# Windowed attention in groups of six query blocks instead of four, with ScalarE's sums of exponentials, shared copies, loads in two parts and ranks from a table

## The chip, the core and the metric

The kernel runs on one core of a Trainium2 chip. Its engines are TensorE (PE in the profile; PEld is its weight load), VectorE (DVE), ScalarE (ACT), GpSimd (POOL) and SyncE (SP), which here only issues the DMAs. The metric is device time in microseconds of one launch: the median of three runs of the kernel before is 353.84 us (353.21 to 354.48).

## The reference

Three layers follow each other. The first is attention for 2 batches of 8 heads, 768 positions, head size 64: each position sees its neighbours closer than 16 and 24 summaries, one for each run of 32 positions (the maximum of the keys, the mean of the values).

```python
k_sum = k.reshape(B, H, nb, block, D).max(axis=3)          # block = 32, nb = 24
v_sum = v.reshape(B, H, nb, block, D).mean(axis=3)
scores_l_m = np.where(mask_l, scale * q @ k.T, -1e9)       # |i - j| < 16
scores_s = scale * einsum('bhsd,bhnd->bhsn', q, k_sum) + np.log(block)
a = softmax(concatenate([scores_l_m, scores_s], axis=-1))
attn = a @ concatenate([v, v_sum], axis=2)
# then, on x of (2, 768, 512)
h = relu(x @ w_in); u, v = halves of h; v_n = layer norm of v
x = (u * (w_spatial @ v_n + b_spatial)) @ w_out
h = relu(x @ w_in2); x = (h * sigmoid(conv3(h))) @ w_out2
```

## The kernel before

Everything after the attention is dense products in three passes of TensorE (high x high, high x low, low x high, lines 274 to 276), 1416 matmuls in all. They are called dense here; 936 of them are 512 columns wide, 480 are 256 wide.

The attention goes by pairs of heads: n = 0 to 7, four pairs for each batch. A pair has 12 query blocks of 64 rows. Each block has 96 keys in its window and 24 summaries, so 120 columns. GB = 4 blocks make a group, NG = 3 groups make a pair; there are 24 groups. A group goes through this chain (function `group`): `qk` writes masks, logarithms and scores into one of two score tiles in PSUM (TensorE, lines 402, 406, 413); `row_max` (VectorE, 417); `exps`, one ScalarE instruction for each of four half-filled tiles of 120 columns (421); `total`, a sum over 484 columns (VectorE, 424), which also takes up a column of 1e-9; `recip` (427); `normalise` (GpSimd, 430); four transposes into the PSUM tile pt (434); a copy of pt to memory (ScalarE, 452); `pv`, the product with the values, into xp (439); the high part of the result (ScalarE, 454) and its low part (VectorE, 455). The results X are the input of the dense products `f1u` and `f1v`: `f1u(0)` needs all four pairs of batch 0.

Around the groups stand, for each pair: the load of keys and queries (`load_kq`, lines 320 and 323) and of values, already laid out in windows (`vwin`, line 330, 576 KB in one DMA); the scaled key windows (GpSimd, 339); the maxima of the keys (VectorE, 344) and their spreading (347); the means of the values. In batch 0 TensorE computes the means from vwin (line 362, 12 blocks one after another), in batch 1 VectorE adds up a second load of the values (line 369). ScalarE copies them (373), GpSimd spreads them over the blocks of each group (376). Buffers alternate between pairs: pair n + 2 is loaded into the places of pair n. Beside all this the first weight matrix `w_in` is loaded and converted in eight pieces (`convert`, lines 259 to 265, then 250 and 244).

A planner (`Plan.order`) sets the order of instructions on every engine before the program is built: each step has a list of engines with a cost, a rank, and what it reads and writes; the step that can start earliest is taken, and among those within 0.1 us the one of the lowest rank. Dense work has ranks from 1000 up, so that it fills TensorE where attention has nothing ready. The chip runs each engine's instructions in that order. The DMAs stand in one queue on SyncE, in order too; an issue waits until its buffer is free.

Of the kernel before, what the change touches and what calls it, by code (L numbers as in the profile page):

```python
# [27 lines left out]
GB = 4  # L28
NG = NB // GB
MK = 4 * NK + 2 * QB + 2 * NS  # L30
# [6 lines left out]
SLOT = 1536  # L37


class Plan:  # L40

# [8 lines left out]
    def add(self, on, rank, reads=(), writes=(), lock=False, mode=None):  # L50
# [20 lines left out]
        self.work.append((on, rank, deps - {k}, lock, mode))  # L71

    def order(self):
# [13 lines left out]
        while ready:  # L87
            best = []
            for k in ready:
                on, rank, deps, lock, mode = self.work[k]  # L90
                for e in on:
                    s = free.get(e, 0.0)
                    for j in deps:
                        t, by = end[j]
                        s = max(s, t + (self.LAND if by == "Q" else 0.0 if by == e else self.HAND))
# [73 lines left out]
def block_kernel(ctx, tc, q_in, k_in, vwin, v_in, mask, runs, w_in, w_spT, b_sp, w_outT, w_in2, conv, w_out2, out):  # L169
# [8 lines left out]
    STEP = 3.0  # L178
# [59 lines left out]
    def dma(kb, fn, rank, reads=(), writes=()):  # L238
        add({"Q": (kb / 265.0, fn)}, rank, reads, writes)
# [65 lines left out]
    def e3(j):  # L305
        return es[j].ap[:, :GB * (NK + 1)].rearrange("p (b k) -> p b k", k=NK + 1)

    def st3(j):
        return sts[j].ap[:, :3 * GB].rearrange("p (b k) -> p b k", k=GB)

# [6 lines left out]
    def load_kq(n):  # L317
        j, r = n % 2, STEP * NG * n
        b, p = divmod(n, NP)
        dma(400, lambda: SP.dma_start(kts[j].f(), k_in[b, p]), r - 12, writes=[kts[j].tok()])  # L320
        cuts = [(0, 256), (256, S)] if n == 0 else [(0, S)]
        for i, (q0, q1) in enumerate(cuts):
            dma((q1 - q0) / 2, lambda q0=q0, q1=q1: SP.dma_start(qts[j].ap[:, q0:q1], q_in[b, p][:, q0:q1]), r - 9 + 1.5 * i, writes=[qts[j].tok(q0, q1)])

    def load_values(n):
        j, r = n % 2, STEP * NG * n
        b, p = divmod(n, NP)
        if b:
            dma(384, lambda: SP.dma_start(vts[j].f(), v_in[p]), r - 7, writes=[vts[j].tok()])
        dma(576, lambda: SP.dma_start(vw3(j)[:WK], vwin[b, p]), r - 6, writes=[vws[j].tok(sub="w")])  # L330

    def keys(n):

        j, r = n % 2, STEP * NG * n
        for g in range(NG):
            def win(g=g):
                t = kts[j].ap
                src = bass.AP(tensor=t.tensor, offset=t.offset + g * GB * QB, ap=[list(t.ap[0]), [QB, GB], [1, WK]])
                POOL.tensor_scalar(out=kw3(j)[:, g * GB:(g + 1) * GB, :WK], in0=src, scalar1=SCALE, scalar2=0.0, op0=ALU.mult, op1=ALU.add)

            add({"POOL": (0.5, win)}, r - 4 + STEP * g, [kts[j].tok(g * GB * QB, (g + 1) * GB * QB + 32)], [kw_tok(j, g)], lock=True)

        def top():
            DVE.tensor_reduce(out=kss[j].ap[:, :NS], in_=kts[j].ap[:, 16:16 + S].rearrange("p (n k) -> p n k", k=32), op=ALU.max, axis=AX.X)
# [5 lines left out]
        add({"DVE": (0.94, top)}, r - 4, [kts[j].tok()], [kss[j].tok()])  # L350
        add({"POOL": (0.46, lambda: put(POOL))} if n else {"DVE": (0.33, lambda: put(DVE))}, r - 3, [kss[j].tok()], [kws[j].tok(sub="s")], lock=True)

    def means(n):
# [3 lines left out]
        if not b:  # L357
            ps, m = mms[1][:NK, :128], tok("mm1")
            for g in range(NG):
# [4 lines left out]
                add({"PE": (0.97, mm)}, r + 1, [vws[j].tok(sub="w"), runs_t.tok()], [m], mode="F")  # L364
# [16 lines left out]
    def xh(b, p, lo, hi):  # L381
        return X[b][p].tok(lo, hi)
# [418 lines left out]
```

## Time and profile before

| | |
|---|---|
| median of 3 runs | 353.84 us |
| the profiled execution: time, span | 351.99 us, 350.2 us |
| TensorE busy | 336.9 us, 96% |
| VectorE, ScalarE, GpSimd busy | 237.0, 185.1, 85.4 us |
| DMA in queue q1 | 33.49 MB, 30.1% of 16 engines' span |

The span goes from the first to the last instruction of the profiled execution. A share of busy time is an average over stages: the attention, up to about 93 us, where all engines work, and the dense rest. TensorE's matmuls overlap, so what one of them costs is read from the distance between two starts, not from its duration. Rows of the timeline begin with the start and the time from start to end; rows of the chain of waits list what released the next piece of work.

### The profile page before, as it was taken

The numbers are of one execution on the slowest core, as the hardware profiler recorded it, in microseconds if no ns is written. First come the engines' busy times: TensorE is split into PE (matmuls) and PEld (weight loads), VectorE is DVE, ScalarE is ACT, GpSimd is POOL, SyncE is SP. The second block draws the span as 40 slices with busy tenths as digits, with TensorE's granted clock in tenths as the row PEclk, the third lists the DMA queues.
The fourth block names the chain that finished last, engine by engine and source line by source line (L and its number), as shares of the span: only waits on it lengthen the run. The fifth ranks groups of instructions, "written<-read, shape, count | busy, mean of one in ns | idle before, by whom it ended". The sixth has DMA issues, their size and how long they took to land.

```text
span 350.2 us, 6496 instructions
## 1 busy us (share of the span) xinstructions
PE 336.9 (96%) x2591; PEld 282.4 (81%) x2591; DVE 237.0 (68%) x400; ACT 185.1 (53%) x374; POOL 85.4 (24%) x117
## 2 busy tenths in 40 slices
PE   7899798799999999999999999999999999999996
PEld 3867675578888888888889888888888888888886
DVE  3799888787378888899896848799885343371000
ACT  3587688687444765434331444888864434451101
POOL 3789787687224002201001020000000000000000
PEclk9999999999999999999999999999999999999999
DMA  7978976622113652032321234000000000001101
GB/s 229 319 243 281 304 216 167 188 70 62 61 61 107 220 162 86 0 104 86 112 71 52 79 102 120 0 2 0 2 1 30 32 30 30 32 1 60 60 32 60
DMA packets 11262, 33.90 MB, mean 97 GB/s; under 512 B 1504, under 2 KB 2016, under 8 KB 11232
## 3 DMA queue, kind: packets, MB, share of 16 engines
q1 hardware_dynamic: 11232, 33.49, 30.1%
q8 instruction: 20, 0.33, 0.4%
q14 instruction: 10, 0.08, 0.1%
HBM read 30.34 MB, written 3.15 MB: 96 GB/s over the span
## 4 chain that ended last, share of the span: by engine, by line
PE 84%; DMA 8%; ACT 3%; DVE 2%; POOL 1%; issue 1%; SPq 0%; ACTq 0%; DVEq 0%; POOLq 0%
PE late L275 12%; PE late L274 12%; PE late L276 12%; PE mm L274 8%; PE mm L275 8%; PE mm L276 8%; DMA a<-vwin 4%; PE xp L275 3%; PE xp L274 3%; PE xp L276 3%; PE mm L362 3%; PE pt L275 3%; PE pt L274 3%; PE pt L276 3%; PE xp L439 2%; DMA a<-w_in 2%
## 5 line engine op out<-in xcount | busy, mean ns | idle before, releaser
L615 DVE SCALAR_TENSOR_TENSOR x<-x,conv_t 128x767 f32<-128x767 f32 x32 | 32.4, 1016 | 16.8 <-ACT x L612 16.6
L421 ACT ACTIVATE a<-s,a 128x120 f32<-128x120 f32 x96 | 26.7, 370 | 7.8 <-DVE a L417 7.6
L260 ACT ACTIVATE a<-a 128x512 f32<-128x512 f32 x28 | 18.9, 676 | 16.3 <-POOL a L244 5.3
L430 POOL TENSOR_TENSOR a<-a,a 128x480 f32<-128x480 f32 x24 | 23.9, 996 | 7.9 <-ACT a L421 4.7
L263 DVE SCALAR_TENSOR_TENSOR a<-a,a 128x512 uint32<-128x512 uint32 x28 | 20.4, 729 | 5.2 <-ACT a L260 4.1
L621 DVE TENSOR_TENSOR x<-x 128x768 f32<-128x768 f32 x16 | 15.3, 957 | 9.0 <-ACT x L618 8.9
L499 POOL TENSOR_TENSOR stat<-stat,mhalf 128x1 f32<-128x1 f32 x12 | 10.5, 873 | 44.8 <-DVE stat L496 44.8
L265 DVE SCALAR_TENSOR_TENSOR a<-a,a 128x512 uint32<-128x512 uint32 x28 | 20.5, 732 | 0.7
L439 PEld LDWEIGHTS xp<-a,a 120*64 120x64 f32 x384 | 13.3, 137 | 9.3 <-POOL a L376 3.0
L439 PE MATMUL xp<-a,a 120*64 120x64 f32 x384 | 16.4, 228 | 3.5 <-POOL a L376 1.7
L618 ACT ACTIVATE x<-x 128x768 f32<-128x768 f32 x16 | 13.5, 841 | 11.7 <-DVE x L615 11.7
L376 POOL TENSOR_SCALAR a<-a 24x512 f32<-24x512 f32 x24 | 16.6, 693 | 7.7 <-ACT a L373 6.2
L417 DVE TENSOR_REDUCE a<-s 128x4 f32<-128x480 f32 x24 | 15.2, 638 | 4.5 <-PE s L413 4.5
L424 DVE TENSOR_REDUCE a<-a 128x4 f32<-128x484 f32 x24 | 15.6, 649 | 2.1 <-ACT a L421 1.6
L434 PE MATMUL pt<-ident,a 128*120 128x128 f32 x96 | 15.2, 281 | 1.6 <-POOL a L430 1.5
L244 POOL TENSOR_TENSOR w<-a,w 128x512 fp32r<-128x512 f32 x9 | 11.5, 1275 | 19.1 <-ACT w L250 19.1
L640 ACT COPY tmp<-late 128x512 f32<-128x512 f32 x7 | 4.1, 587 | 22.7 <-PE late L276 22.7
L274 PE MATMUL mm<-x,w 128*128 128x256 f32 (+1 forms) x40 | 15.6, 389 | 0.3 <-ACT v L515 0.3
L455 DVE TENSOR_TENSOR x<-xp,x 128x256 fp32r<-128x256 f32 x24 | 10.0, 418 | 8.5 <-ACT x L454 8.4
L452 ACT COPY a<-pt 120x512 f32<-120x512 f32 x24 | 14.2, 594 | 2.8 <-PE pt L434 2.6
L274 PE MATMUL mm<-w,x 128*128 128x512 f32 x40 | 15.7, 392 | 0.0
L276 PE MATMUL mm<-w,x 128*128 128x512 f32 x40 | 15.6, 389 | 0.0
(295 smaller groups left out, 1075.5 us busy)
## 6 DMA issues: line engine op xcount, KB each, us to landing
a<-w_in SPq DMA_DIRECT2D x16, 512.0 KB, 4.3
a<-vwin SPq DMA_DIRECT2D x8, 576.0 KB, 6.0
a<-w_out SPq DMA_DIRECT2D x8, 512.0 KB, 3.6
a<-k_in SPq DMA_DIRECT2D x8, 400.0 KB, 3.9
out<-tmp SPq DMA_DIRECT2D x11, 256.0 KB, 2.0
a<-q_in SPq DMA_DIRECT2D x7, 384.0 KB, 6.2
tmp<-w_spT SPq DMA_DIRECT2D x6, 384.0 KB, 3.8
a<-w_outT SPq DMA_DIRECT2D x4, 512.0 KB, 3.9
```

What stands on the lines that cost most here:

```text
L260: add({"ACT": (0.68, lambda: ACT.mul(fu.f(), half(1).bitcast(F32), 2.0 ** -112))}, rank, [raw.tok()], [fu.tok()])
L263: add({"DVE": (0.69, lambda: DVE.scalar_tensor_tensor(out=last.u(), in0=fu.u(), scalar=0x80000000, in1=last.u(), op0=ALU.bitwise_and, op1= ...
L265: add({"DVE": (0.69, lambda: DVE.scalar_tensor_tensor(out=fu.u(), in0=fu.u(), scalar=3, in1=last.u(), op0=ALU.logical_shift_left, op1=ALU. ...
L274: PE.matmul(ps, lhsT=lh, rhs=rh, start=first and i == 0, stop=False)
L275: PE.matmul(ps, lhsT=lh, rhs=rl, start=False, stop=False)
L276: PE.matmul(ps, lhsT=ll, rhs=rh, start=False, stop=last and i == n - 1)
L376: POOL.tensor_scalar(out=vw3(j)[WK:NK, g * GB:(g + 1) * GB], in0=vss[j].ap[WK:NK].unsqueeze(1).to_broadcast([NS, GB, 128]), scalar1=1.0, s ...
L421: ACT.activation(out=e[:, u, :NK], in_=sv[:, u // 2, u % 2], func=AF.Exp, bias=st[:, 0, u:u + 1])
L424: DVE.tensor_reduce(out=st[:, 1], in_=e, op=ALU.add, axis=AX.X)
L430: POOL.tensor_tensor(out=e[:, :, :NK], in0=e[:, :, :NK], in1=st[:, 2].unsqueeze(2).to_broadcast([128, GB, NK]), op=ALU.mult)
L439: PE.matmul(xp[h * D:(h + 1) * D, k * QB:(k + 1) * QB], lhsT=vw3(j)[:NK, g * GB + k, h * D:(h + 1) * D], rhs=pts[:NK, 256 * h + 128 * (k / ...
L615: DVE.scalar_tensor_tensor(out=ct.f()[:, to], in0=hh.f()[:, of], scalar=conv_t[:, 3 * f + k:3 * f + k + 1], in1=ct.f()[:, to], op0=ALU.mul ...
```

## The change

GB goes from 4 to 6: 16 groups of six blocks, two for each pair. A group has three blocks side by side in each half of the score tile (GA = 3), six exponentials, six transposes in two halves of three that use the same part of pt one after the other, each half with a copy of its own. The exponentials give their sums as accumulator outputs; VectorE's `total` then adds only the sum and the 1e-9 of each block (12 numbers). Copies of pt and the high part of the result may go to ScalarE or VectorE, the normalising to GpSimd or VectorE, key windows and spreading of means to GpSimd or ScalarE, low parts of weights to VectorE or GpSimd. TensorE computes the means of pairs 0 and 1 only; from pair 2 on VectorE adds up the second load of the values. In batch 0 keys, queries and vwin are loaded in two parts each. Two tables, SHIFT and PICK, change ranks and fix the engine of single steps of the planner.

```diff
-GB = 4
+GB = 6
+GA = GB // 2
+MEANS_PE = (0, 1)
+SHIFT = (
+    "YYHDBIKKdNCAAKKdiEMucfejQJEfadUhADmQZTDURBAAqLisGARFbFNFJgVKANHhUupWfUntjlLrPsdOKtBbbEsSewBaCCFQJsWKiFsGMEAOSVAAcCoQoJfr"
...
+PICK = (
+    "------------------------01------1--------1---0------0---0-----------------10------0------0-1-0-0----------0-------------"
...
-        self.work.append((on, rank, deps - {k}, lock, mode))
+        if k < len(PICK) and PICK[k] != "-":
+            on = dict([list(on.items())[int(PICK[k])]])
+        self.work.append((on, rank + 0.5 * (SIGNS.index(SHIFT[k]) - 24 if k < len(SHIFT) else 0), deps - {k}, lock, mode))
...
-        if b:
-            dma(384, lambda: SP.dma_start(vts[j].f(), v_in[p]), r - 7, writes=[vts[j].tok()])
-        dma(576, lambda: SP.dma_start(vw3(j)[:WK], vwin[b, p]), r - 6, writes=[vws[j].tok(sub="w")])
+        if n not in MEANS_PE:
+            dma(384, lambda: SP.dma_start(vts[j].f(), v_in[b, p]), r - 7, writes=[vts[j].tok()])
+        parts = NG if n < NP and VPART else 1
+        for i in range(parts):
+            b0, b1 = NB // parts * i, NB // parts * (i + 1)
+            dma(48 * (b1 - b0), lambda b0=b0, b1=b1: SP.dma_start(vw3(j)[:WK, b0:b1], vwin[b, p][:, b0:b1]), r - 6 + 0.5 * i,
+                writes=[vws[j].tok(b0 * 128, b1 * 128, "w")])
...
-        if not b:
+        if n in MEANS_PE:
...
-                ACT.activation(out=e[:, u, :NK], in_=sv[:, u // 2, u % 2], func=AF.Exp, bias=st[:, 0, u:u + 1])
+                ACT.activation(out=e[:, u, :NK], in_=sv[:, u // GA, u % GA], func=AF.Exp, bias=st[:, 0, u:u + 1], scale=1.0, accum_out=sm[:, u, :1])
...
-            DVE.tensor_reduce(out=st[:, 1], in_=e, op=ALU.add, axis=AX.X)
+            DVE.tensor_reduce(out=st[:, 1], in_=sm, op=ALU.add, axis=AX.X)
...
-        add({"POOL": (1.02, normalise)}, r + 3.5, [st_], [e_], lock=True)
-        add({"PE": (0.46, transposes)}, r + 4.6, [e_], [tok("pt")], mode="F")
-        add({"ACT": (0.6, lambda: ACT.copy(pts[:NK], pt[:NK]))}, r + 5.1, [tok("pt")], [pts_])
-        add({"PE": (0.6, pv)}, r + 5.8, [pts_, vw_tok(j, g, "w"), vw_tok(j, g, "m")], [tok("xp")], mode="P")
-        add({"ACT": (0.4, lambda: ACT.copy(hi, xp[:, :GB * QB]))}, r + 6.5, [tok("xp")], [xh(b, p, t0, t1)])
+        add({"POOL": (1.5, normalise), **({"DVE": (0.91, lambda: normalise(DVE))} if NORM else {})}, r + 4.5, [st_], [e_], lock=True)
+        for h in range(2):
...
+            add({"PE": (0.37, lambda h=h: transposes(h))}, r + 6 + 0.5 * h, [e_], [tok("pt")], mode="F")
+            add({"ACT": (0.52, lambda copy=copy: copy(ACT)), **({"DVE": (0.53, lambda copy=copy: copy(DVE))} if FLEX else {})}, r + 6.5 + 0.5 * h, [tok("pt")], [part.tok()])
+        add({"PE": (0.88, pv)}, r + 7.5, [pts_, vw_tok(j, g, "w"), vw_tok(j, g, "m")], [tok("xp")], mode="P")
+        add({"ACT": (0.52, lambda: ACT.copy(hi, xp[:, :GB * QB])), **({"DVE": (0.53, lambda: DVE.tensor_copy(hi, xp[:, :GB * QB]))} if FLEX else {})}, r + 8.5, [tok("xp")], [xh(b, p, t0, t1)])
```

Three places show how the order moves. The first is SyncE's queue of loads in batch 0; before, a5 holds the values of pairs 1 and 3, a11 those of pairs 0 and 2, and each pair has one vwin.

```order
L330 DMA a5_0_210<-vwin 96x1536
L320 DMA a7_0_96<-k_in 128x800
L323 DMA a6_0_128<-q_in 128x768
L259 DMA a1_0_247<-w_in 128x1024
L320 DMA a13_0_99<-k_in 128x800
L259 DMA a0_0_195<-w_in 128x1024
L323 DMA a12_0_183<-q_in 128x768
L330 DMA a11_0_134<-vwin 96x1536
```

In the changed kernel a2 holds the values of pairs 0 and 2, a3 those of pairs 1 and 3; these rows go from pair 1's values to pair 2's.

```order
L380 DMA a3_0_297<-vwin 96x768 x2
L370 DMA a7_0_219<-q_in 128x384
L376 DMA a6_0_130<-v_in 128x768
L299 DMA a1_0_352<-w_in 128x1024
L299 DMA a0_0_194<-w_in 128x1024
L370 DMA a6_0_130<-q_in 128x384
L367 DMA a8_0_95<-k_in 128x800
L370 DMA a7_0_219<-q_in 128x384
L380 DMA a3_0_297<-vwin 96x768
L380 DMA a2_0_133<-vwin 96x768 x2
```

The loads come in halves; a second load of values (v_in) for pairs 2 and 3 is new in batch 0; the first half of pair 3's vwin now stands ahead of both halves of pair 2's.

The second place is TensorE at the means of pair 2; before, twelve products with vwin as their input stand between a value product (439) and the next transposes.

```order
L413 MATMUL s_0_80<-a10_0_94,a6_0_128 64x120 x8
L439 MATMUL xp_83<-a13_0_99,a5_0_210 64x64 x8
L362 MATMUL mm_1_85<-a11_0_134,a3_0_86 120x128 x12
L434 MATMUL pt_82<-ident_65,a2_0_95 120x128 x4
```

In the changed kernel one transposition of VectorE's sums stands for them, and dense products (314 to 316) follow.

```order
L476 MATMUL s_1_81<-a5_0_98,a7_0_219 64x120 x12
L497 MATMUL pt_82<-ident_65,a8_0_95 120x128 x3
L432 MATMUL xp_83<-ident_65,a12_0_86 120x128
L314 MATMUL mm_1_85<-x01_0_101,w0_0_327 128x512
L315 MATMUL mm_1_85<-x01_0_101,w0_0_327 128x512
L316 MATMUL mm_1_85<-x01_0_101,w1_0_509 128x512
```

TensorE no longer waits for vwin there, but for the smaller load of v_in by way of VectorE.

The third place is ScalarE's start; before, the exponentials of two groups are followed by copies and conversions only.

```order
L421 ACTIVATE a2_0_95<-s_0_80,a10_0_94 128x120 x4
L421 ACTIVATE a2_0_95<-s_1_81,a4_0_98 128x120 x4
L373 ACTIVATE a7_0_96<-mm_1_85 24x128
L452 COPY a7_0_96<-pt_82 120x512
L260 ACTIVATE a1_0_247<-a0_0_195 128x512
L454 CAST x00_0_97<-xp_83 128x256
```

In the changed kernel key windows (392) and the spreading of means (438) stand there too.

```order
L484 ACTIVATE a8_0_95,a4_0_94<-s_0_80,a4_0_94 128x120 x6
L484 ACTIVATE a9_0_99,a5_0_98<-s_1_81,a5_0_98 128x120 x6
L392 ACTIVATE a5_0_98<-a9_0_99 128x6x96
L300 ACTIVATE a0_0_194<-a0_0_194 128x512
L433 ACTIVATE a11_0_100<-mm_1_85 24x128
L438 COPY a2_0_133<-a11_0_100 24x768
L392 ACTIVATE a4_0_94<-a8_0_95 128x6x96
L519 COPY a10_0_96<-pt_82 120x384
```

Six exponentials now have a second output each, and three steps of GpSimd (one spreading, two windows) have come to ScalarE ahead of its first copy of pt.

## Rows read from the trace of the kernel before

**Rows 1.** The page, its first part: busy us, share, instructions.

```profile
PE 336.9 (96%) x2591; PEld 282.4 (81%) x2591; DVE 237.0 (68%) x400; ACT 185.1 (53%) x374; POOL 85.4 (24%) x117
```

**Rows 2.** Busy time by stretches: stretch, length, engines, granted clock, DMA share, GB/s.

```profile
4.90:52.30 47.40, 41.81 (x722) 33.60 (x722) 39.33 (x76) 32.16 (x94) 36.87 (x49) 1.00 0.86 272
52.30:93.20 40.90, 37.24 (x542) 28.91 (x540) 30.07 (x61) 29.18 (x83) 29.18 (x37) 1.00 0.38 107
93.20:347.30 254.10, 254.00 (x1324) 218.50 (x1320) 166.25 (x261) 122.14 (x197) 16.88 (x17) 1.00 0.19 61
```

**Rows 3.** Chain of waits, 20 to 70 us: start, length, what.

```profile
21.87 6.40 DMA a<-vwin
...
28.31 2.88 PE mm L362 x24
...
33.03 6.48 DMA a<-vwin
...
39.55 2.88 PE mm L362 x24
...
49.37 5.70 DMA a<-k_in
...
60.23 5.95 DMA a<-w_in
```

**Rows 4.** Timeline of PE, four short stretches: start, length, instructions.

```profile
9.08 2.85 PE L362 MATMUL mm<-a,a 96*120 96x128 f32 x24 [1.33 <-DVE a L424]
11.77 0.60 PE L434 MATMUL pt<-ident,a 128*120 128x128 f32 x4
12.30 0.30 PE L402 MATMUL s<-a 64*64 64x240 bf16 x4
...
13.14 0.69 PE L439 MATMUL xp<-a,a 120*64 120x64 f32 x16
13.75 0.30 PE L402 MATMUL s<-a 64*64 64x240 bf16 x4
...
24.70 0.30 PE L402 MATMUL s<-a 64*64 64x240 bf16 x4
...
25.39 0.38 PE L274 MATMUL mm<-x,w 128*128 128x256 f32 x1
...
92.62 0.69 PE L439 MATMUL xp<-a,a 120*64 120x64 f32 x16
93.23 0.50 PE L274 MATMUL mm<-w,x 128*128 128x512 f32 x1
93.57 0.39 PE L275 MATMUL mm<-w,x 128*128 128x512 f32 x1
93.80 0.39 PE L276 MATMUL mm<-w,x 128*128 128x512 f32 x1
```

**Rows 5.** Timeline of ACT, from its first exponentials.

```profile
7.17 2.12 ACT L421 ACTIVATE a<-s,a 128x120 f32<-128x120 f32 x8 [5.18 <-DVE a L417]
...
19.51 0.27 ACT L373 ACTIVATE a<-mm 24x128 f32<-24x128 f32 x1
19.80 0.68 ACT L260 ACTIVATE a<-a 128x512 f32<-128x512 f32 x1
20.50 0.59 ACT L452 COPY a<-pt 120x512 f32<-120x512 f32 x1
21.09 1.11 ACT L421 ACTIVATE a<-s,a 128x120 f32<-128x120 f32 x4
22.08 0.39 ACT L454 CAST x<-xp 128x256 fp32r<-128x256 f32 x1
22.54 0.59 ACT L452 COPY a<-pt 120x512 f32<-120x512 f32 x1
23.02 0.68 ACT L260 ACTIVATE a<-a 128x512 f32<-128x512 f32 x1
```

**Rows 6.** Groups by line: shapes, count, busy us, mean ns, idle before.

```profile
L424 DVE TENSOR_REDUCE a<-a 128x4 f32<-128x484 f32 x24 | 15.6, 649 | 2.1 <-ACT a L421 1.6 <-POOL a L430 0.2
```

More of the change, by code (lines that the diff above doesn't have):

```diff
@@ L335, in keys, with win, top @@
         for g in range(NG):
-            def win(g=g):
+            def win(eng, g=g):
                 t = kts[j].ap
                 src = bass.AP(tensor=t.tensor, offset=t.offset + g * GB * QB, ap=[list(t.ap[0]), [QB, GB], [1, WK]])
[L339 to L344, printed above, removed]
+                dst = kw3(j)[:, g * GB:(g + 1) * GB, :WK]
+                if eng is ACT:
+                    ACT.mul(dst, src, SCALE)
+                else:
+                    eng.tensor_scalar(out=dst, in0=src, scalar1=SCALE, scalar2=0.0, op0=ALU.mult, op1=ALU.add)
+            add({"POOL": (0.8, lambda win=win: win(POOL)), "ACT": (0.7, lambda win=win: win(ACT))}, r - 4 + STEP * g,
+                [kts[j].tok(g * GB * QB, (g + 1) * GB * QB + 32)], [kw_tok(j, g)], lock=True)
+        parts = 2 if n < NP and KPART else 1
+        for i in range(parts):
+            def top(i=i, w=S // parts):
+                DVE.tensor_reduce(out=kss[j].ap[:, w // 32 * i:w // 32 * (i + 1)], in_=kts[j].ap[:, 16 + w * i:16 + w * (i + 1)].rearrange("p (n k) -> p n k", k=32), op=ALU.max, axis=AX.X)
+            w = S // parts
+            add({"DVE": (0.14 + w / 960, top)}, r - 4, [kts[j].tok(16 + w * i, 16 + w * (i + 1))], [kss[j].tok(w // 32 * i, w // 32 * (i + 1))])
         def put(eng):
@@ L398, in qk @@
             for c in range(2):
-                at = NK if c == 0 and g else 2 * NK if c == 1 and g == NG - 1 else 0 if c == 0 else NK
+                at = 0 if c == 0 and g == 0 else 2 * NK if c == 1 and g == NG - 1 else NK
                 for h in range(2):
                     rows = slice(h * D, (h + 1) * D)
-                    PE.matmul(s[c * QB:(c + 1) * QB, h, :2 * NK], lhsT=one[rows], rhs=masks[rows, at:at + 2 * NK], start=True, stop=False, skip_group_check=True)
+                    PE.matmul(s[c * QB:(c + 1) * QB, h, :GA * NK], lhsT=one[rows], rhs=masks[rows, at:at + GA * NK], start=True, stop=False, skip_group_check=True)
             for c in range(2):
@@ L407, in qk @@
                               start=False, stop=True, skip_group_check=True)
-            for a in range(2):
+            for a in range(GA):
                 for c in range(2):
@@ L763 @@
             vwin[:, :, at:at + hi - lo, b, j * D:(j + 1) * D] = vh[:, :, j, lo:hi]
[L764 to L765 removed]
+    vin = pairs_T(v)
+    mask = np.zeros((QB, 5, NK), f32)
     bf16 = mybir.dt.np(mybir.dt.bfloat16)
@@ L769 @@
             inside = 1 <= c - p <= 31
-            for m, ok in enumerate((inside and c >= 16, inside, inside, inside and c < QB + 16)):
+            for m, ok in enumerate((inside and c >= 16, inside, inside, inside, inside and c < QB + 16)):
                 mask[p, m, c] = 0.0 if ok else -1.0e9
     weight = f32(math.log(32))
-    logs, three = np.zeros((QB, 2 * NS), f32), np.zeros((QB, QB), f32)
+    logs, three = np.zeros((QB, GA * NS), f32), np.zeros((QB, QB), f32)
     for r in range(3):
@@ L781 @@
         runs[16 + j * 32:48 + j * 32, j] = 1.0 / 32.0
-    mask = np.concatenate([mask.reshape(QB, 4 * NK), np.eye(QB, dtype=f32), three, logs], axis=1)
+    mask = np.concatenate([mask.reshape(QB, 5 * NK), np.eye(QB, dtype=f32), three, logs], axis=1)
     mask = np.concatenate([mask, mask], axis=0).astype(bf16)
```

135 lines of the change are left out of this document (88 added, 47 removed).

## The prediction, on record before the changed kernel ran

> **What bounds the kernel now.** I read the page's busy shares first, then busy time by stretches, the chain of waits, and the timelines of TensorE and ScalarE. TensorE is busy 96% of the span [rows 1]. The stretches say where the other 4% lie: from 93.2 to 347.3 us it is busy 254.0 of 254.1 us; from 4.9 to 52.3 us it is idle 47.40 - 41.81 = 5.6 us, from 52.3 to 93.2 us 40.90 - 37.24 = 3.7 us [rows 2]. 52.3 is where batch 0's attention ends, 93.2 where the last value product does. [...] In the first stretch VectorE is busy 39.3 us, GpSimd 36.9, ScalarE 32.2, and the DMA engines 86% at 272 GB/s: everything is near its limit and nothing is at it. The chain of waits tells why TensorE waits there: twice a vwin takes 6.4 and 6.5 us from issue to landing, and 2.88 us of means stand behind each [rows 3]. Later a k_in (5.7 us) and a w_in (6.0 us) do the same, in the second stretch.
>
> So the time follows from P, the end of the last value product (93.2 now), and the dense work that is left then, which runs without a gap. By the order 1320 of the 1416 dense matmuls are left now and 1284 in the changed kernel. A matmul of 512 columns takes 0.23 us from start to start [rows 4], so 36 fewer shorten the rest by 8.3 us. No change of time means P = 93.2 + 8.3 = 101.5 us.
>
> **The change, part by part, on TensorE up to P.** Busy time there is 41.8 + 37.2 = 79.0 us, before it 4.9 us.
> - Means of pairs 2 and 3: two sets of twelve blocks go. A set takes 11.77 - 9.08 = 2.69 us [rows 4]: -5.4 us. Two more transpositions of sums, 0.13 us each at the rate of the four at 11.77: +0.3.
> - Transposes: 96 as before, but 32 batches of three for 24 of four. Four take 0.53 us with one change of layout [rows 4]. At a cost per transpose nothing changes; at a cost per batch it is 8 x 0.53 = +4.2. I take +1.5, nearer the first, since a matmul's price in these rows goes by its columns.
> - Scores: four blocks take 25.39 - 24.70 = 0.69 us [rows 4]. 16 groups of six at 1.04 or 24 of four at 0.69 are both 16.6 us; were the cost one per group, 5.5 us would go. I take 0, the value by columns. Value products (13.75 - 13.14 = 0.61 for four) by the same rule: 0.
> - 36 more dense matmuls ahead of P: +8.3.
> - The start: mask and first queries are larger; I take +0.3 us, a DMA of 0.1 MB at 272 GB/s.
>
> Work up to P is then 4.9 + 79.0 - 5.4 + 0.3 + 1.5 + 8.3 + 0.3 = 88.9 us, and P = 88.9 + idle. Against 101.5 the change of time is idle - 12.6 us. With today's idle of 9.3 us that is -3.3; so the question is TensorE's idle time in the new attention.
>
> **Idle in batch 0.** It ends with the eighth value product. TensorE's own work up to there: 4.9 + 41.8 - 5.4, with some 0.7 for transposes, 1.0 for one batch of scores more (66 blocks ahead for 60), 1.0 for six dense matmuls with their changes of layout: 44.0 us. ScalarE is the engine that gains work. From its first exponentials at 7.2 us to the last copy of the eighth group its order holds 54 exponentials (nine groups), 4 scalings and 3 casts of weights, 4 copies of means, 12 copies of 384 columns, 3 key windows and 4 spreadings. Four exponentials take 22.08 - 21.09 = 0.99 us, a scaling 0.70, a copy of means 0.29, a copy of 512 columns 0.48 (22.54 to 23.02), so one of 384 about 0.40 [rows 5]; a cast is priced as a scaling; the windows (576 columns) and spreadings (768) as one grown by the columns, 0.75 and 0.95. Sum: 13.4 + 4.9 + 1.2 + 4.8 + 6.1 = 30.4 us, and the value product follows 1.0 us behind: 38.6 us, plus 54 accumulator outputs.
>
> No row shows such an output. Its bounds: nothing, if it rides along, or 0.29 us, the distance that the smallest ScalarE instruction of these rows takes (line 373, 24 x 128). I take 0.10, nearer to the free end, because in rows 5 all but a small part of a copy's time goes with its columns and an accumulator has one. That gives 38.6 + 5.4 = 44.0 us: the same as TensorE. [...]
>
> VectorE stays level: it loses the long sums, 0.649 us each [rows 6], twelve of them in batch 0 (7.8 us), and takes 11 copies of 384 columns, two normalisings and sums of values. GpSimd loses work. Two engines that both need 44 us, each waiting for the other within a group, don't end at 44: before, TensorE filled 41.81 of 47.40 us, 88%. I take 90% of the 39.1 us behind the start and get 4.9 + 39.1/0.90 = 48 us; since the two vwin waits go (the halves are freed by the pair's first group, and the means no longer stand behind them), I take 47.5, an idle of 3.5 us. What is late next is ScalarE's copy of pt behind windows and spreadings.
>
> **Idle in batch 1.** TensorE has dense work to put between, ScalarE and VectorE have slack (29.2 and 30.1 of 40.9 us now). The 3.7 us were mostly behind the two loads of rows 3; these now start earlier in the queue. I take 2.8. Idle is 6.3 in all, the change -6.3 us.
>
> **The dense rest.** By the order GpSimd gets ten 768-column steps there (six low parts, four gates) that VectorE had. VectorE is busy 166 of 254 us in that stretch and TensorE waits for 0.1 [rows 2], so I cost it at nothing; without that cover each step is late by its own length at most.
>
> **The sum.** The profiled execution took 351.99 us (span 350.2 and 1.8 around it), 1.85 below the median of 353.84; I take the difference off the median: 353.84 - 6.3 = 347.5 us.
>
> **The rivals.**
> - The accumulator outputs bind ScalarE (slower). If each is an instruction of its own at 0.29 us, batch 0 ends at 38.6 + 15.7 + 3.5 = 57.8 us, idle there is 13.8, the change 13.8 + 2.8 - 12.6 = +4.0: 357.8 us. For it: there is no row on such an output, and ScalarE issues the six of a group in a row while VectorE waits. Against: today it is the emptiest of the compute engines in batch 0. It turns into a loss above about 0.21 us each. [...] Chance 14%.
> - The loads decide again, so that idle stays 9.3 us: 353.84 - 3.3 = 350.5 us. For it: 86% DMA share at 272 GB/s, two loads of v_in more (0.79 MB, 2.9 us at that rate), and in the queue pair 2's values wait behind half of pair 3's, which wait for the third value product. Against: by the order 9.5 MB stand ahead of the last value of batch 0, 35 us at that rate, and that value is needed only after 42. Chance 21%.
> - ScalarE and TensorE mesh well and the accumulator is nearly free: batch 0 ends near 45, idle is 2 in all, -10.6: 343.2 us. For it: the loads' halves go ahead of the means, and ScalarE's free time today is 15 us of 47 [rows 2]. Against: no stretch of the attention got beyond 91% on TensorE. Chance 15%.
> - My forecast, -4 to -9 us: 48%. The rest, 2%, is a wait in the dense part.
>
> **How the numbers follow.** The likeliest case gives 347.5 us. Below it the range reaches to the well-meshed case with the transposes at no extra cost (343.2 - 1.5, to 341.2), above it to idle as before with the accumulator at 0.20 us, which is no change (353.8). A change of 0.3%, 1.1 us, is about what a measurement of this kernel can tell from none. Faster: 48 + 15 and nearly all of the second case and of outputs between 0.10 and 0.2 us, 0.81; same 0.05; slower 0.14.
>
> **What would show it.** Right: no 2.9 us of means after the second set, the last value product ending near 95 us, TensorE idle near 6 us before that and none behind it, exponentials less than 0.4 us apart, no vwin on the chain for 6 us. Wrong: ScalarE busy above 95% from 7 us to the end of batch 0 with TensorE waiting for its copies of pt (the first rival), or vwin or v_in on the chain again (the second). The forecast falls altogether if the dense part shows gaps.

## Result and profile after

The changed kernel takes 342.77 us in the median of 4 runs (342.26 to 343.95), the kernel before 353.9 us (353.21 to 354.48, 4 runs): a ratio of 0.969 (95% interval 0.966 to 0.972). On another chip it was 343.09 against 353.63 us, 0.973 (0.970 to 0.977). The forecast was 347.5 us, so direction and range were right and the gain, 11.1 us by the medians, was nearly twice the 6.3 us forecast; it lies outside the band of 4 to 9 us that the forecast called its own. The profiled executions differ by 9.73 us (351.99 and 342.26 us), their spans by 9.7 (350.2 and 340.5 us). The other 1.4 us lie between a profiled execution and its median: 1.9 us before, 0.5 us now.

The page's busy shares, the counterpart of [rows 1], then its rows of TensorE's busy share and of the granted clock in 40 slices of 8.5 us (each digit in tenths, 9 for 90% or more):

```profile
PE 329.2 (97%) x2481; PEld 275.5 (81%) x2481; DVE 239.3 (70%) x389; ACT 190.3 (56%) x458; POOL 92.3 (27%) x90
...
PE   7999789998999999999999999999999999999996
...
PEclk9999999999999999999999999999999999999999
```

Busy time by stretches, cut at the same events as [rows 2] (the end of the eighth value product and of the last one; columns as there):

```profile
4.90:47.90 43.00, 38.52 (x674) 29.04 (x673) 35.91 (x73) 37.82 (x154) 23.46 (x25) 1.00 0.89 276
47.90:91.50 43.60, 41.07 (x516) 33.35 (x516) 40.58 (x79) 33.65 (x116) 18.41 (x18) 1.00 0.50 159
91.50:337.60 246.10, 245.78 (x1286) 211.68 (x1284) 161.45 (x235) 117.46 (x191) 48.50 (x33) 1.00 0.18 61
```

Batch 0 ends at 47.9 us (forecast 47.5, before 52.3). TensorE idles 43.00 - 38.52 = 4.5 us in it and 43.60 - 41.07 = 2.5 us in batch 1, 7.0 in all (forecast 6.3, before 9.3). P, the end of the last value product, is 91.5 us (forecast some 95, before 93.2). Behind it nothing waits: 245.78 of 246.10 us are busy.

The longest loads on the chain of waits, where [rows 3] had two vwin of 6.4 and 6.5 us:

```profile
3.50 5.63 DMA a<-k_in
...
34.37 10.59 DMA a<-w_in
...
61.54 5.72 DMA a<-w_in
```

No vwin is among them. The w_in of 10.59 us is new there, and the last w_in starts no earlier than before (60.23 us in [rows 3]); no run moves these two. ScalarE's first exponentials, the counterpart of [rows 5] (start, length, line, operation):

```profile
8.64 0.36 ACT L484 ACTIVATE a<-s,a 128x120 f32<-128x120 f32 x1 [2.98 <-DVE a L480]
8.90 0.19 ACT L484 ACTIVATION_READ_ACCUMULATOR a<-s,a 128x1 f32 x1
8.99 0.35 ACT L484 ACTIVATE a<-s,a 128x120 f32<-128x120 f32 x1
9.23 0.20 ACT L484 ACTIVATION_READ_ACCUMULATOR a<-s,a 128x1 f32 x1
9.33 0.36 ACT L484 ACTIVATE a<-s,a 128x120 f32<-128x120 f32 x1
```

The accumulator output is an instruction of its own here. From one exponential to the next it is 0.34 us now (9.33 - 8.99) and was 0.25 [rows 5], so an output costs 0.09 us. The row's own length of 0.2 us is not its price, since most of it lies beside its neighbours (8.90 + 0.19 = 9.09, and the next exponential starts at 8.99).

TensorE at two groups of batch 0, the counterpart of [rows 4]:

```profile
14.31 0.35 PE L465 MATMUL s<-a 64*64 64x360 bf16 x4
14.49 0.20 PE L469 MATMUL s<-a 64*64 64x72 bf16 x4
14.52 0.81 PE L476 MATMUL s<-a,a 64*64 64x120 f32 x24
15.27 0.54 PE L497 MATMUL pt<-ident,a 128*120 128x128 f32 x3
15.74 0.35 PE L465 MATMUL s<-a 64*64 64x360 bf16 x4
```

A batch of six scores takes 15.27 - 14.31 = 0.96 us where the forecast had 1.04, three transposes 15.74 - 15.27 = 0.47 us; four took 0.53 [rows 4].

### The profile page after: what moved, and what is told of

The parts are those of the page before. It is cut to its first block, busy times and chain, and to the rows that moved or that the text cites. A ratio compares the mean times of both kernels' runs of the same rounds, so it can differ in the third digit from the quotient of the medians.

```text
span 340.5 us, 6306 instructions
## 1 busy us (share of the span) xinstructions
PE 329.2 (97%) x2481; PEld 275.5 (81%) x2481; DVE 239.3 (70%) x389; ACT 190.3 (56%) x458; POOL 92.3 (27%) x90
## 4 chain that ended last, share of the span: by engine, by line
PE 80%; DMA 6%; DVE 5%; ACT 4%; SPq 1%; issue 1%; POOL 1%; DVEq 0%; ACTq 0%
PE late L315 12%; PE late L314 12%; PE late L316 12%; PE mm L314 8%; PE mm L315 7%; PE mm L316 7%; DMA a<-w_in 5%; PE xp L315 3%; PE xp L314 3%; PE xp L316 3%; PE pt L315 3%; PE pt L316 3%; PE pt L314 3%; ACT a L484 2%; PE mm L422 2%; DMA a<-k_in 2%
## 5 line engine op out<-in xcount | busy, mean ns | idle before, releaser
L685 DVE SCALAR_TENSOR_TENSOR x<-x,conv_t 128x767 f32<-128x767 f32 x32 | 37.9, 1200 | 16.3 <-ACT x L682 16.0
L484 ACT ACTIVATE a<-s,a 128x120 f32<-128x120 f32 x96 | 33.3, 380 | 3.4 <-DVE a L480 3.0
L484 ACT ACTIVATION_READ_ACCUMULATOR a<-s,a 128x1 f32 x96 | 21.7, 226 | 0.0
L493 POOL TENSOR_TENSOR a<-a,a 128x720 f32<-128x720 f32 x11 | 16.2, 1477 | 16.8 <-DVE a L490 8.5
L284 POOL TENSOR_TENSOR a<-a,a 128x512 fp32r<-128x512 f32 x6 | 8.6, 1427 | 33.7 <-issue 18.0
L480 DVE TENSOR_REDUCE a<-s 128x6 f32<-128x720 f32 x16 | 14.4, 899 | 3.0 <-PE s L476 3.0
L314 PE MATMUL mm<-w,x 128*128 128x512 f32 x40 | 16.2, 405 | 0.0
L682 ACT ACTIVATE x<-x,conv_t 128x768 f32<-128x768 f32 x16 | 15.0, 938 | 1.6 <-DVE w L284 0.7
L316 PE MATMUL mm<-w,x 128*128 128x512 f32 x40 | 15.6, 391 | 0.0
L315 PE MATMUL mm<-w,x 128*128 128x512 f32 x40 | 15.6, 390 | 0.0
L497 PEld LDWEIGHTS pt<-ident,a 128*120 128x120 f32 x96 | 10.3, 137 | 6.4 <-issue 2.7
L290 ACT CAST w<-a 128x512 fp32r<-128x512 f32 x16 | 10.1, 630 | 9.1 <-DVE a L305 9.1
```

Source lines behind the costliest of these rows:

```text
L284: eng.tensor_tensor(out=lo.r(), in0=src.f(), in1=hi.f(), op=ALU.subtract)
L314: PE.matmul(ps, lhsT=lh, rhs=rh, start=first and i == 0, stop=False)
L315: PE.matmul(ps, lhsT=lh, rhs=rl, start=False, stop=False)
L316: PE.matmul(ps, lhsT=ll, rhs=rh, start=False, stop=last and i == n - 1)
L484: ACT.activation(out=e[:, u, :NK], in_=sv[:, u // GA, u % GA], func=AF.Exp, bias=st[:, 0, u:u + 1], scale=1.0, accum_out=sm[:, u, :1])
L493: eng.tensor_tensor(out=e, in0=e, in1=st[:, 1].unsqueeze(2).to_broadcast([128, GB, NK]), op=ALU.mult)
```

## Experiments

One equation ran through the prediction: the time is P plus the dense matmuls that are left then. It was not given as an equation with a constant, but the runs allow one. In the table "left" is the number of dense matmuls behind P, and "sum" is P + 248.9 + 0.22 x (left - 1284), with 248.9 and 1284 from the changed kernel; 0.22 us is what each of the 36 more takes behind P in the kernel before. P, left and span are those of the profiled execution.

| kernel | P | left | sum | span | median, ratio to before |
|---|---|---|---|---|---|
| before | 93.2 | 1320 | 350.0 | 350.2 | 353.9 |
| changed | 91.5 | 1284 | 340.4 | 340.5 | 342.77, 0.969 |
| e1_products_back | 96.5 | 1284 | 345.4 | 345.5 | 349.74, 0.984 |
| e3_sums_by_vector | 100.7 | 1284 | 349.6 | 349.6 | 352.45, 0.994 |
| e4_no_tables | 90.2 | 1317 | 346.4 | 346.6 | 348.43, 0.986 |
| e5_no_tables_fours | 101.1 | 1296 | 352.6 | 352.7 | 354.44, 1.004 |
| e6_mask_first | 92.8 | 1284 | 341.7 | 341.7 | 343.58, 0.968 |
| e7_loads_whole | 94.8 | 1320 | 351.6 | 351.9 | 355.20, 1.010 |
| e8_means_alone | 94.6 | 1317 | 350.8 | 351.0 | 351.71, 0.995 |
| e9_mean1_by_vector | 104.0 | 1311 | 358.8 | 358.9 | 359.27, 1.018 |
| e10_no_fillers | 92.3 | 1284 | 341.2 | 341.2 | 343.58, 0.976 |
| e11_two_waits | 91.9 | 1284 | 340.8 | 340.8 | 342.46, 0.971 |
| e12_whole_same_order | 95.2 | 1284 | 344.1 | 344.1 | 345.44, 0.977 |

The sum meets the span within 0.3 us in all thirteen. Whatever an edit did, it did to P or to the number of dense matmuls put ahead of it. By this equation a dense matmul ahead of P gains its 0.22 us only where it fills a wait; elsewhere it makes P later by about as much. The runs were made on several chips, on which before took 354.75 us (e1, e3, e6), 353.5 (e4, e5, e8, e9), 353.63 (e7, e10, e11, after_again) and 353.72 (e12).

**e1_products_back.** TensorE gets back the products of the means of pairs 2 and 3, with constants in place of vwin so that they wait for nothing new.

```diff
+            def tr():
+                if n in (2, 3):
+                    for blk in range(NB):
+                        PE.matmul(ps, lhsT=runs_t.ap[:WK, NZ - WK - 2 * blk:NZ - WK - 2 * blk + NK], rhs=ident[:WK, :128], start=blk == 0, stop=blk == NB - 1)
+                PE.transpose(ps, vzs[j].ap[:, :NK], ident)
...
```

> The changed kernel, with 24 more products of 96 x 120 by 128 columns on TensorE, twelve each in front of the transposed sums of pairs 2 and 3, the places in batch 0 where the means stood before. They read constants, so they wait for no load; their results are overwritten. Theory A (TensorE's own work up to the last value product is what the time is made of; its idle time does not take up new work): 24 x 0.225 = 5.4 us more, less about 1 us of idle that stands beside these places: 346.2 to 348.2 us. Rival B (ScalarE and the loads set when batch 0 ends, TensorE's extra work goes into its idle time): 342.8 to 344.8 us.

P went from 91.5 to 96.5 us and the ratio is 0.984 (0.978 to 0.990). The 5.4 us of the prediction's term passed on as 5.0: work of TensorE ahead of P counts nearly in full. The profiled execution, 347.33 us at a clock of 1.00, is theory A's; the median, 349.74, is above it, and the other three executions had a mean clock of 0.990 to 0.995.

**e3_sums_by_vector.** The accumulator outputs go, VectorE sums the exponentials itself.

```diff
-                ACT.activation(..., bias=st[:, 0, u:u + 1], scale=1.0, accum_out=sm[:, u, :1])
+                ACT.activation(..., bias=st[:, 0, u:u + 1], scale=1.0)
...
-            DVE.tensor_reduce(out=st[:, 1], in_=sm, op=ALU.add, axis=AX.X)
+            DVE.tensor_reduce(out=st[:, 1], in_=e, op=ALU.add, axis=AX.X)
```

> The changed kernel in the same order, but the exponentials have no accumulator output, and VectorE adds up all 720 columns of a group (the 1e-9 is left out of the sum). ScalarE loses 96 x 0.09 = 8.8 us, half of it in batch 0; VectorE gains 16 x 0.75 = 12 us, 6 of it in batch 0, where it is busy 35.9 of 43.0 us. Theory A (VectorE is the scarcer of the two, the accumulators pay): 345 to 348.5 us. Rival B (ScalarE's accumulators hold up batch 0 and cost more than they save): 340 to 342.5 us.

352.45 us, ratio 0.994 (0.990 to 0.997): slower than the changed kernel by more than theory A had. Its two stretches up to P:

```profile
4.90:51.70 46.80, 39.46 (x678) 29.89 (x680) 42.45 (x73) 33.73 (x95) 23.64 (x25) 0.96 0.82 254
51.70:100.70 49.00, 43.42 (x516) 34.37 (x514) 46.42 (x79) 30.40 (x77) 18.37 (x18) 0.97 0.45 141
```

ScalarE loses 4.1 us of 37.82 in batch 0, VectorE gains 6.5 and is busy 46.42 of 49.00 us in batch 1. TensorE idles 7.3 + 5.6 us instead of 7.0. The clock is the second part: 0.96 and 0.97 where it was 1.00. The outputs were the cheap side of this exchange.

**e4_no_tables and e5_no_tables_fours.** SHIFT and PICK are empty, so the planner goes by its own ranks and costs; e5 also goes back to groups of four, with the costs and ranks of four.

```diff
-SHIFT = (
...
+SHIFT = ""
+PICK = ""
...
-GB = 6
+GB = 4
...
```

> The changed kernel with SHIFT and PICK empty: the planner's own ranks and engines, everything else as it is. Theory A (the new shape of the attention carries the gain: fewer products of means, cheaper batches of scores, no waits behind whole vwin loads; the tables add a part): 344 to 349 us, with the means' 5.4 us gone in any case. Rival B (the tables carry it; without them the copies and loads stand in each other's way and idle time is as before or longer): 350 to 357 us.

> As the kernel without tables, but in groups of four: GB = 4, 24 groups, with the planner's costs of the steps cut to size; accumulators, shared copies, parts of loads and VectorE's means stay. Theory A (scores are cheaper in batches of six: 16 batches instead of 24 save some 2 us of TensorE's work, and transposes and value products 1 us): 2 to 5 us above the kernel in sixes without tables. Rival B (the size of the group matters little, since columns make the price): within 1 us of it.

Without the tables it is 348.43 us, ratio 0.986 (0.981 to 0.992). P is even 1.3 us earlier, but 33 dense matmuls fewer stand ahead of it. In fours the same plan takes 354.44 us, ratio 1.004 (1.001 to 1.007), 6 us more: P goes up 10.9 us, and 21 dense matmuls are put ahead. That is above theory A's 2 to 5 us. So the six blocks are worth some 6 us under one set of rules, and the tables about as much again, by filling dense work into the attention. Without both, the rest of the change (accumulators, shared copies, VectorE's means, halves of loads) gains nothing: 354.44 us against 353.5 before. The shared copies were not taken out by themselves.

**e6_mask_first.** In the changed kernel the first scores start at 6.60 us and wait for the mask. Here it is loaded ahead of the first queries.

```diff
...
+        done.remove(mask_job)
+        done.insert(done.index(q[2]), mask_job)
+        done.remove(q[4])
+        done.insert(done.index(q[5]) + 1, q[4])
```

> The changed kernel with one edit in SyncE's queue: the mask goes ahead of the first queries, and the first part of pair 0's values goes behind their second part. The first scores began at 6.60 us, 1.6 us later than before, and waited for the mask. Theory A (the start is on the path: ScalarE begins its exponentials behind it and is nearly full from there on): scores at 5.6 to 6.1 us, 341.6 to 342.3 us. Rival B (batch 0 is set by loads further back in the queue, the start is hidden): within 0.2 us of 342.8.

343.58 us, ratio 0.968 (0.963 to 0.973): no change that can be told. The scores start 0.4 us earlier, then wait 0.54 us for the queries, and P is 1.3 us later.

**e8_means_alone.** The kernel before, with one part of the change: VectorE computes the means of pairs 2 and 3.

```diff
-        if b:
-            dma(384, lambda: SP.dma_start(vts[j].f(), v_in[p]), r - 7, writes=[vts[j].tok()])
+        if n >= 2:
+            dma(384, lambda: SP.dma_start(vts[j].f(), v_in[b, p]), r - 7, writes=[vts[j].tok()])
...
-        if not b:
+        if n < 2:
...
```

> The kernel before with one part of the change alone: pairs 2 and 3 have their means summed by VectorE from a second load of the values, not by 24 products on TensorE behind the whole vwin. Theory A (TensorE's work is paid for, and both waits for vwin of 6.4 us leave the chain): 5 to 8 us below the kernel before. Rival B (the value products wait for the same vwin soon after, and the two loads of v_in cost DMA time in the stretch that is 86% full): 0 to 3 us below.

351.71 us, ratio 0.995 (0.991 to 0.999): 1.7 us by the medians, as rival B had it, although 5.4 us of work are gone; the profiled execution is no faster than that of the kernel before (span 351.0 and 350.2 us). The page's rows of it:

```profile
PE   7897669999999999999999999999999999999996
...
PEclk9899996999999999999999999999999999999999
```

TensorE's busy share falls to 0.6 in the fifth and sixth slice (35 to 53 us), and the row of the granted clock shows 6 tenths in the seventh slice behind them (52.7 to 61.4 us); over 52.3 to 94.6 us the clock is 0.93. Up to P TensorE idles 12.3 us, 3.1 more than before, the longest time for a VectorE step:

```profile
53.49 1.12 PE L439 MATMUL xp<-a,a 120*64 120x64 f32 x16 [3.21 <-DVE a L427]
```

The value products and dense matmuls there take longer, and only 99 dense matmuls stand ahead of P.

**e9_mean1_by_vector.** The changed kernel, with the means of pair 1 by VectorE too.

```diff
-MEANS_PE = (0, 1)
+MEANS_PE = (0,)
...
```

> The changed kernel with the means of pair 1 by VectorE too (MEANS_PE = (0,)), so that only pair 0's stay on TensorE; the tables' rows are kept in step, the new load has none. Theory A (TensorE's work in batch 0 passes on in full, as 24 added products did): 2.7 us of products go, 339.5 to 341.5 us. Rival B (the loads at the start are the limit: 0.39 MB more ahead of pair 1's values, 1.4 us at 274 GB/s, takes it back): 342 to 344.5 us.

359.27 us, ratio 1.018 (1.012 to 1.024): slower than before, and both theories missed by some 15 us or more. The same two rows show both reasons:

```profile
PE   6997949796899999999999999999999999999996
...
PEclk9899887898999999999999999999999999999999
```

With less to do TensorE waits more (busy 0.4 in the sixth slice), and the clock is under 0.9 in six of the first ten slices. Its plan also puts 105 dense matmuls ahead of P, not 132. Up to P TensorE idles 18.0 us, 11.0 more than in the changed kernel; that is the larger part of the 18.4 us by which the sum grows. The other 7.4 us are work that takes longer, although 2.9 us of means are gone: the clock over 4.9 to 103.9 us is 0.90 (were it 0.50 each time it fell, as from 7.7 to 11.0 us here, that would be a fifth of the time, an estimate). Its two longest waits, 3.3 and 2.7 us, are for copies of pt on ScalarE and VectorE; why those come late was not tested.

**e7_loads_whole and e12_whole_same_order.** The values of pairs 1 to 3 are loaded whole. In e7 the plan is made anew; in e12 the whole load stands where the second half stood, and nothing else moves.

```diff
-        parts = NG if n < NP and VPART else 1
+        parts = NG if n == 0 else 1
...
```

> The values of pairs 1 to 3 are loaded whole again instead of in two parts; the two tables that shift ranks and choose engines keep their entries for every other piece of work, and the plan is made anew. Theory A (a half can start when the first group of the pair before has been used up, so the parts take a wait off TensorE): the vwin loads are on the chain of waits again, TensorE's idle time before the last value product grows by 1 to 4 us, and the time is 1 to 4 us above the changed kernel's. Rival B (the loads start early enough in either form): the time is within 1 us of the changed kernel's and no vwin is on the chain for over 3 us.

```diff
+            def part(b0=b0, b1=b1):
+                if b1 == NB:
+                    b0 = 0 if n else b0
+                    SP.dma_start(vw3(j)[:WK, b0:b1], vwin[b, p][:, b0:b1])
+                elif n == 0:
+                    SP.dma_start(vw3(j)[:WK, b0:b1], vwin[b, p][:, b0:b1])
...
```

> The values of pairs 1 to 3 are loaded whole at the place in the queue where the changed kernel loads their second half; nothing is planned anew, every other instruction stands where it stands in the changed kernel. Theory A (what e7_loads_whole lost is the loads themselves: a whole load waits until the pair before is used up, and TensorE waits for it): a vwin stands on the chain of waits, the last value product ends 2 us or more later than in the changed kernel (91.5 us), and the time is 345 us or more. Rival B (e7_loads_whole lost by its new plan, which puts only 96 of the dense products ahead of the last value product in place of 132; the loads come early enough in either form): 132 dense products stay ahead, the last value product ends within 1 us of 91.5, and the time is 342 to 344 us.

e7 takes 355.2 us, ratio 1.010 (1.004 to 1.016), far above theory A: its plan has only 96 dense matmuls ahead of P, as before the change, and its clock is 0.90 in batch 1. Alone it could not say what the halves are worth. e12 can: 345.44 us, ratio 0.977 (0.972 to 0.983), against 342.77 to 343.09; theory A, with a vwin of 5.85 us on the chain of waits. TensorE at the means of pair 1, in the changed kernel and then in e12:

```profile
18.36 0.54 PE L497 MATMUL pt<-ident,a 128*120 128x128 f32 x3 [0.28 <-DVE a L519]
18.94 2.88 PE L422 MATMUL mm<-a,a 96*120 96x128 f32 x24
```

```profile
18.18 0.54 PE L504 MATMUL pt<-ident,a 128*120 128x128 f32 x3 [0.19 <-DVE a L526]
20.70 4.55 PE L429 MATMUL mm<-a,a 96*120 96x128 f32 x24 [1.98 <-DMA a<-vwin]
```

The whole load comes 2.0 us late, and the same products then take 4.55 us instead of 2.88. The longer products go with the clock: over 20.70 to 25.30 us it is granted at 0.63 there and at 1.00 in the changed kernel.

```profile
20.70:25.30 4.60, 4.60 (x28) 4.47 (x30) 2.17 (x6) 1.19 (x9) 1.57 (x2) 0.63 1.02 394
```

At the end of these products e12 is (20.70 + 4.55) - (18.94 + 2.88) = 3.4 us behind the changed kernel, at P 95.2 - 91.5 = 3.7 us. So the wait of 2.0 us cost nearly twice its length. It doesn't do so in each execution: of the six of e12, two have a mean clock of 1.000 and take 343.65 and 344.71 us; the other four, at 0.990 to 0.995, take 345.03 to 347.61.

**e10_no_fillers.** The planner puts eight matmuls of constants into TensorE's waits after the first scores. They are left out, the order is kept.

```diff
-        for *_, fn in done:
-            fn()
+        for t, k, e, us, fn in done:
+            if e != "PE" or "<lambda>" not in fn.__name__ or fn.__defaults__ is None or len(fn.__defaults__) != 2:
+                fn()
```

> The eight filler matmuls on the tile of ones that the plan puts into TensorE's waits after the first scores are left out; every other instruction stands in the same order. Their results are used by nothing. Theory A (what TensorE does in its waits holds the granted clock): the granted clock shows a stretch at its half level between 5 and 25 us, and the time is 1 to 4 us above the changed kernel's. Rival B (the clock is held by the real work, the fillers only fill): the clock stays at 1.00 and the time is within 0.5 us of the changed kernel's.

343.58 us against 343.09 on the same chip, ratio 0.976 (0.971 to 0.981): not to be told apart. The clock has a stretch at half its level, 0.50 from 7.10 to 10.50 us, as theory A had it, and the time is theory B's. TensorE at the first scores, then the stretches around them:

```profile
7.00 0.46 PE L465 MATMUL s<-a 64*64 64x360 bf16 x4 [2.12 <-DMA a<-mask]
```

```profile
4.90:7.10 2.20, 0.10 (x4) 0.11 (x8) 0.15 (x1) 0.81 (x2) 0.00 (x0) 1.00 1.00 278
7.10:10.50 3.40, 3.27 (x64) 2.68 (x62) 1.43 (x3) 0.73 (x5) 0.21 (x1) 0.50 1.06 284
10.50:17.00 6.50, 5.53 (x94) 4.78 (x94) 5.50 (x13) 6.42 (x26) 3.13 (x4) 1.00 0.66 231
```

This doesn't show that the fillers hold the clock. It falls at 7.1 us, behind a wait of 2.12 us for the mask (0.69 us in the changed kernel's trace), and the first filler that was left out stood behind the scores that start here. e9 has its fillers in place, waits 2.13 us for the mask, and its clock is 0.50 from 7.7 to 11.0 us. What speaks for the fillers is the mean clock of whole executions: four of the six here have 0.985 to 0.995, and all ten of the changed kernel 0.998 or more. P is only 0.7 us later.

**e11_two_waits.** An attempt at a better version: the small tile for the means is loaded earlier and copied by GpSimd, and one copy of pt goes from VectorE to ScalarE, which idles there. TensorE waited 0.70 and 1.01 us at these places.

```diff
...
+        for x, y in ((q[8], q[3]), (run_job, [x for x in done if x[2] == "POOL"][1])):
+            done.remove(x)
+            done.insert(done.index(y) + 1, x)
...
-                (ACT.copy if eng is ACT else DVE.tensor_copy)(part.ap[:NK], pt[:NK, :128 * GA])
+                (ACT.copy if eng is ACT or (i, h) == MOVED else DVE.tensor_copy)(part.ap[:NK], pt[:NK, :128 * GA])
```

> The changed kernel once more, on the chip on which the next three run, so that they are compared with it there. Both theories expect 342 to 344 us and a ratio to before near 0.969.

> Two waits of TensorE in the changed kernel's trace are taken away in it, everything else stands in the same order: the small tile of runs is loaded right behind the mask and copied by GpSimd instead of VectorE (the first means wait 0.70 us behind that copy), and the copy of transposed exponentials at 80.94 us goes from VectorE, where 2.5 us of integer steps and casts stand ahead of it, to ScalarE, which idles there (TensorE waits 1.01 us behind it). Theory A (a wait that goes ahead of the last value product is a gain in full): the last value product ends 1.0 to 1.7 us earlier and the time falls by 1.0 to 1.7 us. Rival B (the next wait takes its place, as when the mask was loaded first): under 0.6 us.

342.46 us against 343.09, ratios 0.971 (0.967 to 0.975) and 0.973 (0.970 to 0.977): no difference that can be told, rival B. The two places in it:

```profile
11.18 2.85 PE L422 MATMUL mm<-a,a 96*120 96x128 f32 x24 [0.74 <-POOL a L408]
...
81.96 0.52 PE L497 MATMUL pt<-ident,a 128*120 128x128 f32 x3 [0.53 <-ACT a L519]
```

The first wait is still there with another engine's name on it, although the copy now ends at 6.4 us; so the copy was not what it waited for. A second profile of the unedited changed kernel (after_again) puts this wait, 0.85 us there, down to a vwin:

```profile
11.35 2.85 PE L422 MATMUL mm<-a,a 96*120 96x128 f32 x24 [0.85 <-DMA a<-vwin]
```

The second wait is half as long. P is 91.9 us, not earlier.

## Why the prediction was right, and where it was off

**The time** came near the third rival's, 343.2 us (15%), and not near the forecast's 347.5, but not by that rival's mechanism: it needed batch 0 to end near 45 us and 2 us of idle time, and 47.9 and 7.0 came. Of the two steps that put the low end of the range there (which add up to 343.2 - 1.5 = 341.7, not 341.2) only one came, transposes at no extra cost. The rest came from scores, value products and the median, below.

**The bound** held: P and what is left behind it set the time, with no gap in the dense part, in every kernel of the table.

**Idle time** held: 4.5 and 2.5 us where 3.5 and 2.8 were forecast, and batch 0 ends at 47.9 us where 47.5 was. The reason given, that the vwin waits go, is half shown: no vwin is on the chain, and e12 shows that the halves take away a wait, but at the means of pair 1. The two waits of [rows 3] were not put back by themselves. What TensorE itself waited for them before was less than the 6.4 and 6.5 us of the chain:

```profile
28.31 2.88 PE L362 MATMUL mm<-a,a 96*120 96x128 f32 x24 [0.41 <-DMA a<-vwin]
...
39.55 2.88 PE L362 MATMUL mm<-a,a 96*120 96x128 f32 x24 [1.94 <-DMA a<-vwin]
```

These 2.4 us are gone, and other waits took 1.3 us of them back.

**Batch 1** was to have slack. ScalarE has it (33.65 of 43.60 us), VectorE doesn't: it goes from 30.07 of 40.90 us [rows 2] to 40.58 of 43.60. TensorE's longest wait there is behind it:

```profile
81.63 0.52 PE L497 MATMUL pt<-ident,a 128*120 128x128 f32 x3 [1.01 <-DVE a L487]
```

With the copies, normalisings and sums of values that it got, VectorE is thus near its limit in batch 1; there dense work fills most of what TensorE would wait.

**The accumulator** held as a number: 0.10 us taken, 0.09 found. The reason for it did not, and the hit was in part luck: all but a small part of a copy's time was said to go with its columns, but by [rows 5] 512 columns take 0.48 us and 128 take 0.29, so some 0.23 us go with none. The 0.20 us for an output at the upper end of the range is in no run; the trace shows 0.09. The rival in which it binds ScalarE needed 0.21. ScalarE is busy 37.82 of 43.00 us in batch 0, and TensorE waits for it 0.5 us at a time at the most.

**TensorE's work up to P** is where the forecast was off: 88.9 us were forecast (with the first 4.9), 91.5 - 7.0 = 84.5 came. By kind, from the start of a batch to the start of the next without the idle time between, summed over all batches up to P:

| kind | before | after | change | forecast |
|---|---|---|---|---|
| means | 11.0 | 5.5 | -5.5 | -5.4 |
| scores | 17.5 | 15.6 | -1.9 | 0 |
| transposes | 12.8 | 12.2 | -0.6 | +1.5 |
| value products | 14.9 | 14.2 | -0.8 | 0 |
| dense ahead of P | 20.5 | 28.6 | +8.1 | +8.3 |
| fillers | 6.0 | 6.9 | +0.9 | 0 |

The terms that failed are "I take 0, the value by columns" for scores and value products, and "+1.5" for transposes. Together they are 4.8 us too high. That a price goes by the columns was the author's reading, which the rows do not show: in [rows 4] a product of the means, 128 columns, takes 0.22 us (2.69/12), a transpose of 128 columns 0.13 (0.53/4), a dense matmul of 512 columns 0.23. Fillers took 0.9 us more than forecast and the smaller terms (start, means, dense work) 0.5 less, so the work is 4.4 us below the forecast; idle time is 0.7 above it, and that leaves the error in P, 95.2 - 91.5 = 3.7 us. Scores are paid partly by group: 17.5/24 = 0.73 us for four blocks and 15.6/16 = 0.98 for six, where 1.5 times 0.73 would be 1.09; the prediction had 0 and -5.5 as their bounds. For transposes the sign was wrong. They are paid one by one, 12.8/96 = 0.13 us before and 12.2/96 = 0.13 now, so eight more batches cost nothing; three beside a change of layout take 0.47 us, but 12.2/32 = 0.38 on the mean.

**The median** adds the last part: the forecast took the difference of profiled executions off the median of before. That difference is 9.7 us and the medians differ by 11.1, so the forecast lost another 1.4 us there.

**What it did not price** is the clock: the sum has no term for it, and the rows come from one execution. In the two profiled executions the clock is 1.00 throughout, but for the kernel before that is the exception: of its 49 executions on four other chips that enter the ratios, 8 have a mean clock of 0.999 or more and take 349.2 to 353.0 us (median 351.0), the other 41 have 0.984 to 0.995 and take 351.7 to 357.2 us (median 353.7). All ten executions of the changed kernel have 0.998 or more. So part of the gain by the medians is clock that the kernel before loses and the changed one keeps. On the chip of the result itself the clock of the kernel before is on record for the profiled execution alone, so that the 1.4 us above are this cause is likely and not shown.

Nor does the prediction ask what happens to the clock if a new order waits longer. In e8 and e9 longer waits and a lower clock together made a gain small (12.3 us idle, 0.96 up to 52.3 us and 0.93 from there to 94.6, ratio 0.995) or turned it into a loss (18.0 us idle, 0.90, ratio 1.018). The changed kernel avoids both, and its tables take part in that: with them empty the clock from 4.9 to 50 us is 0.92 (e4_no_tables).

```profile
4.90:50.00 45.10, 36.51 (x606) 28.63 (x605) 37.93 (x74) 33.81 (x136) 22.13 (x25) 0.92 0.89 270
```

## What to carry to other kernels

Where a stage that waits is followed by dense work that doesn't, find the event that ends the waiting; what counts is its time and how much of the dense work is ahead of it. A price read at one group size can't tell what goes by the group from what goes by the column, so keep both bounds where the size changes. Taking work off the busiest engine can lose time, as in e9, where 2.9 us of work went, that engine waited 11.0 us more at a clock of 0.90, and the ratio went from 0.969 to 1.018; so look at the granted clock of each slice, and at the mean clock of more than one execution, before a gain is believed.

## What the runs showed of the hardware

- In the changed kernel's trace each accumulator output of a ScalarE exponential is an instruction of its own and costs 0.09 us from start to start (exponentials 0.34 us apart with it, 0.25 without in [rows 5]).
- In the profiled executions of eight of the eleven edited kernels (not in e1, e6 and e11) the granted clock was under 0.9 in one to six slices of the attention, and at 0.9 or more in all slices behind it. These eight idle 9.9 to 18.0 us on TensorE up to P; the other three, the kernel before and the changed one idle 6.9 to 9.5. In e12 the clock was 0.63 from 20.70 to 25.30 us, behind a wait of 2.0 us, and the twelve blocks of products there took 4.55 us instead of 2.88, with TensorE busy 4.60 of 4.60 us. In e10 it was 0.50 from 7.10 to 10.50 us, behind a wait of 2.12 us, with TensorE busy 3.27 of 3.40 us. So in these two the lower clock came behind a wait and lasted while TensorE worked again; what sets it was not shown.
- VectorE's 32 taps (line 685, two inputs each) take 1200 ns on the mean, 1016 before. Five of them take over 1.1 us, 1448 to 2657 ns, and each of these starts while a GpSimd step of two inputs runs; four into which such a step falls later take 1012 to 1019. In a stretch of six they take 1017 to 2485 ns; the longest there starts at 301.4 us, 0.3 us after a GpSimd step that the change had moved there.

```profile
L685 DVE SCALAR_TENSOR_TENSOR x<-x,conv_t x6: 1017/1018/2485, 286.5 to 301.4; 128x767 f32<-128x767 f32 x6
```

```profile
301.16 1.95 POOL L284 TENSOR_TENSOR x<-x,x 128x768 fp32r<-128x768 f32 x1 [28.99 <-ACT x L290]
```

It costs nothing here: behind P TensorE is busy 245.78 of 246.10 us.
